# Moving low halves of probabilities to GpSimd, and LayerNorm's centring and the scaling of cumulated sums to ScalarE

## The chip, the cores and the metric

The kernel runs on one core of a Trainium2 chip. A core has five engines that work at the same time, each through its own queue of instructions in the order of the program: TensorE (matmuls, PE in the profile, and PEld for the loading of its weights), VectorE (DVE), ScalarE (ACT), GpSimd (POOL) and SyncE (SP, which here issues nearly all DMAs). An instruction that has to wait for another engine holds up everything behind it on its own engine. The metric is the time of one execution on the device in microseconds (us).

## The reference

Three blocks follow each other. The shapes are 4 batches, 8 heads, 576 positions, 64 numbers per head, so a model width of 512; the hidden width of both MLPs is 2048.

```python
# attention, with a bias from cumulated sums
cum = cumsum(maximum(s, 0))
scores = q @ k.T / 8 + minimum(-(cum[i] - cum[j]), 0), causal
x = softmax(scores) @ v                                  # [4, 576, 512]
# first MLP, after a two-dimensional Fourier transform
u = x + real(fft(fft(x, axis=1), axis=2))
x = u + relu(layernorm(u) @ w_ch1) @ w_ch2
# second MLP
x = x + relu((layernorm(x) * g_ln) @ w_ch1') @ w_ch2'
```

Where the kernel needs more accuracy than fp16 has, it splits an fp32 value into two fp16 numbers: a high half (the value rounded) and a low half (what is left). A product of two such values is then three fp16 matmuls.

## The kernel before, in words

**Stages.** Attention of batch 0 runs first, beside the loading of the first MLP's weights. Then the first MLP works through the batches while the attention and the Fourier transform of the next batch are mixed into it: `Side` hands out pieces of the next batch's work after each step of the MLP. In the profile, MLP of batch 0 runs from about 169 to 308 us beside attention of batch 1, MLP of batch 1 from 310 to 450 beside attention of batch 2, MLP of batch 2 from 460 to 604 beside attention of batch 3, and MLP of batch 3 until about 727 beside the loading, converting and splitting of the second MLP's weights. From there on the second MLP runs alone; it uses a scheme with seven products in place of eight, for which GpSimd makes sums of activations (L461 to L464).

**Attention.** A batch has four pairs of heads; a pair has five tiles of query rows (`A0`, `A1`, `M`, `B1`, `B0`, numbers 0, 1, 2, 3, 4) for each of two heads, 40 units a batch. A tile reaches back over 129, 257, 320, 448 or 576 columns. A unit goes through the engines like this (batches 2 and 3):

- GpSimd writes the masked bias into the unit's fp32 tile (`emit_bias`, L739), three units ahead. It reads the pair's cumulated sums, spread over all rows and multiplied by the pair's scale (`scale_cum`, L655).
- TensorE makes the scores in PSUM (L756, L757; the PSUM pool has three slots), and VectorE adds them to the bias and finds the minimum of a row (L758), which frees the slot.
- ScalarE takes the exponential twice: as fp16, the high half (L781), and as fp32 in place with the sum of a row (L782).
- VectorE or GpSimd subtracts one from the other, which is the low half (`emit_lo`, L794). `KN["LO_POOL"]` lists for each batch the tiles that GpSimd takes; VectorE takes the others. The fp32 tile is free after that, for the bias of a later unit.
- SyncE issues a DMA that transposes both halves (L798, L806), and TensorE multiplies them with v (`emit_pv`, L826), five to seven units after the scores.

**LayerNorm.** `emit_ln` prepares a chunk of one or two tiles of 128 rows for an MLP: mean and variance (L338, L339), a rough reciprocal root `p` (L343), then for each tile the normalized row `un` in fp32, its high half, its low half, and a transposing DMA (L359). A finer factor for the root is applied to the MLP's output. `un` lies in buffers shared with attention; from the second MLP's weights on it has one buffer of its own. The next chunk's LayerNorm is mixed into the steps of the current chunk.

**Order.** A planner orders the instructions of each engine by a simulated time that it works out from costs of its own, by the order of the program and by priorities (`urgent`). All waits between engines follow from the data.

Of the kernel before, what the change touches and what calls it, by code (L numbers as in the profile page):

```python
# [26 lines left out]
EXT = [129, 257, 320, 448, 576]  # L27
NKB = [2, 3, 3, 4, 5]
MASKED = -(2.0 ** 120)
KN = {'PVS': (0, 3, 0, 0), 'ORD': ((0, 0, 0), (0, 0, 0), (1, 0, 0), (1, 0, 0)), 'WR4': (1.2, 1.2, 1.2, 1.2), 'W0': 4, 'WRATE': 1.0, 'W2PRE': 18, 'NCONST': 40, 'HOLDN': 1, 'S1': 4, 'S2': 1, 'S1B': 0, 'COST': (1.0, 1.0, 1.0, 1.0, 1.0), 'POOL1': (), 'POOLB': (0, 1, 2, 3, 4, 5, 6, 7), 'QF': (3, 3, 3, 3, 3, 3, 3, 3, 3, 3, 3), 'QL': (1, 1, 1, 1), 'WCALLS': 2, 'WN': 65, 'SPGATE': 0, 'LATE4': 1, 'MARK': 30, 'CJ': (2, 6), 'PVLAG': 7, 'LOLAG': 1, 'PVLAG32': 5, 'PJ32': 4, 'A0OFF': 0, 'A1OFF': 0, 'F0OFF': 300, 'AOFF': (200, 0, 300, 300), 'FOFF': (300, 600, 300, 150), 'LNOFF': (300, 600, 150, 600), 'LOFF': 300, 'PJ': 1, 'PN': 1, 'PL': 6, 'KPREP': 0, 'KPRE': (6, 0, 0), 'KSTEP': ((0, 0, 1), (0, 1), (1,)), 'RATES': (1.9, 1.4, 2.1, 1.2), 'POOLX': (0, 1, 1, 1), 'LO_POOL': ((0, 4, 1, 3, 2), (0, 1, 2, 3), (4,), (0, 1, 2)), 'TAILW': 2, 'LNM': 0, 'LAZY': 8, 'CALLS3': 65, 'N32': 2}  # L30


@with_exitstack
def fused_kernel(ctx: ExitStack, tc, q, k, v, s, wa1, wa2, g_ln, wb1, wb2, tok_c, feat_c, ident_c, rev_c, bias_c, out):
    nc = tc.nc
# [4 lines left out]
    mpool = ctx.enter_context(tc.tile_pool(name="mpool", bufs=2))  # L40
# [70 lines left out]
    class Weights:  # L111
# [42 lines left out]
        def convert(self, i):  # L154
# [172 lines left out]
    def emit_ln(ch):  # L327

        n = ch.n
        xs = [ch.get(j) for j in range(n)]
        ch.x = xs
        mv = small.tile([128, 2, 2], F32, tag="mv", name="mv")[:, 0:n, :]
        for j in range(n):
            st = small.tile([128, 6], F32, tag="st", name="st")
            nc.vector.bn_stats(out=st, in_=xs[j])  # L338
            nc.vector.bn_aggr(out=mv[:, j, :], in_=st)  # L339
        va4 = small.tile([128, 8], F32, tag="va", name="va")  # L340
        va, p, d, mp = (va4[:, 2 * i:2 * i + n] for i in range(4))
        nc.vector.tensor_scalar(out=va, in0=mv[:, :, 1], scalar1=1e-6, scalar2=None, op0=ALU.add)
        nc.vector.tensor_scalar(  # L343
            out=p.bitcast(I32), in0=va.bitcast(I32), scalar1=-0.5, scalar2=float(0x5F3759DF), op0=ALU.mult, op1=ALU.add
        )
        ch.last = nc.vector.scalar_tensor_tensor(out=mp, in0=mv[:, :, 0], scalar=-1.0, in1=p, op0=ALU.mult, op1=ALU.mult)
        yield
        ch.unT = mpool.tile([128, 8, 256], F16, tag="unT", name="unT")
        for j in range(n):
            un = un_tile[0]()[:, 0:512]  # L350
# [161 lines left out]
    class MlpStream:  # L512
# [5 lines left out]
        def run(self, chunks, side, first_ln=True, last=None):  # L518

            if first_ln:  # L520
                for _ in emit_ln(chunks[0]):
                    pass
            for c, ch in enumerate(chunks):
                nxt = urgent(emit_ln(chunks[c + 1]), KN["LOFF"]) if c + 1 < len(chunks) else None
                seven = isinstance(ch.w, Weights7)
                for m in range(MB // 2) if seven else range(0, MB, 2):
                    if not seven:
                        ch.w.lazy(m)
                    self.pend.append((ch, m, (emit_g1x if seven else emit_g1)(ch, m)))
# [773 lines left out]
    if True:  # L1303
# [59 lines left out]
        for n, _ in enumerate(urgent(emit_ln(first[0]), KN["LNOFF"][0])):  # L1363
            weights_after((list(KN["QL"]) + [0] * 9)[n], first[0].last)
# [110 lines left out]
```

## Time and profile before

| | |
|---|---|
| time, median of three runs | 1094.59 us (1094.49 to 1094.82) |
| the profiled execution's own time | 1095.33 us |
| its span, first to last instruction | 1093.6 us |
| mean granted TensorE clock | 0.95 of full speed |
| TensorE busy | 967.2 us, 8644 matmuls |
| VectorE busy | 720.1 us, 1848 instructions |
| ScalarE busy | 580.1 us, 1350 instructions |
| GpSimd busy | 415.3 us, 717 instructions |

The profile shows one execution. Busy time is time in which an engine worked on an instruction; issuing DMAs and waiting do not count. Matmuls overlap in a pipeline and their ends are modelled, so TensorE can be shown busy while it is not at its peak. The time that an engine sat idle before an instruction is put down to the instruction or DMA that came last among those it waited for. Times in a timeline are counted from the start of the span.

### The profile page before, as it was taken

The page shows a single profiled execution, that of the slowest core. Times are in us where ns is not written, and L with a number is a line of the kernel's source. Part 1 is how long each engine was busy: PE and PEld are TensorE (multiplying, and loading weights), DVE is VectorE, ACT ScalarE, POOL GpSimd, SP SyncE. Part 2 cuts the span into 40 slices and gives each one's busy share as a digit, 9 for nine tenths or more (in the row PEclk, how much of TensorE's full clock was granted, in tenths as well). Part 3 has the DMA queues.
Part 4 walks back from the last instruction along what each step waited for, and adds up shares of the span by engine and source line. Part 5 has one row for each costly group of instructions (what it writes and reads, how often), then busy time and mean ns, then how long its engine had stood idle before and what let it go on. Part 6 is the DMA issues. An engine that isn't in the chain of part 4 may idle for free.

```text
span 1093.6 us, 23078 instructions
## 1 busy us (share of the span) xinstructions
PE 967.2 (88%) x8644; PEld 740.8 (68%) x8644; DVE 720.1 (66%) x1848; ACT 580.1 (53%) x1350; POOL 415.3 (38%) x717
## 2 busy tenths in 40 slices
PE   4676379999888899688999998898999999999998
PEld 3454246776665666455766665576888888888887
DVE  5978998656896664965757599867644644552342
ACT  5778559774776653576622255744333334333341
POOL 3425444544242231323311000467545443543452
PEclk9768578999999999898999999999999999999999
DMA  6999956986579980598904297020211111110000
GB/s 177 277 199 264 241 132 136 177 147 132 112 139 204 167 157 1 122 196 138 190 20 151 68 291 252 21 58 1 59 20 47 52 27 53 40 40 20 20 21 21
DMA packets 291369, 125.48 MB, mean 115 GB/s; under 512 B 272952, under 2 KB 273208, under 8 KB 291256
## 3 DMA queue, kind: packets, MB, share of 16 engines
q1 hardware_dynamic: 290616, 121.90, 49.9%
q0 software_dynamic: 640, 2.10, 0.6%
q8 instruction: 68, 1.11, 0.4%
q14 instruction: 45, 0.37, 0.1%
HBM read 61.50 MB, written 9.51 MB: 65 GB/s over the span
## 4 chain that ended last, share of the span: by engine, by line
PE 38%; DVE 10%; POOL 3%; DMA 2%; ACT 1%; issue 1%; SPq 1%; ACTq 0%
PE acc L481 13%; PE g1x L453 7%; PE g L453 7%; PE g L387 4%; PE g L411 4%; POOL wbsums L304 2%; DVE wbbig L313 1%; DVE wbbig L165 1%; DMA wbbig<-in_moe_w_ch_dram 1%; DVE wbbig L162 1%; PE pv L826 1%; DVE h L394 1%; DVE wb L162 1%; DVE wb L165 1%; SPq L798 1%
## 5 line engine op out<-in xcount | busy, mean ns | idle before, releaser
L387 PE MATMUL g<-unT,wa 128*128 128x256 f16 (+1 forms) x1920 | 219.4, 265 | 1.4 <-DVE h L394 0.8
L411 PE MATMUL g<-wa,h 128*128 128x512 f16 x864 | 207.4, 382 | 9.2 <-DVE h L394 5.1
L387 PEld LDWEIGHTS <-wa 128*128 128x128 f16 x1920 | 173.9, 99 | 39.7 <-issue 3.0
L481 PE MATMUL acc<-wbbig,wa 128*128 128x256 f16 x1512 | 178.5, 273 | 6.6 <-DVE wa L467 5.3
L453 PEld LDWEIGHTS <-wb 128*128 128x128 f16 x1728 | 169.1, 98 | 20.2
L467 DVE TENSOR_TENSOR wa<-wa,wa 128x896 f16<-128x896 f32 x72 | 79.2, 1100 | 149.2 <-ACT wa L466 149.2
L481 PEld LDWEIGHTS <-wa 128*128 128x128 f16 x1512 | 147.3, 98 | 25.7 <-DVE wa L467 6.7
L411 PEld LDWEIGHTS <-h 128*128 128x128 f16 x864 | 82.9, 99 | 92.5 <-DVE h L394 8.6
L466 ACT CAST wa<-wa 128x896 f16<-128x896 f32 x72 | 67.4, 938 | 117.3 <-POOL wa L464 117.3
L794 POOL TENSOR_TENSOR p<-sc,p 128x129 f16<-128x129 f32 (+4 forms) x104 | 94.7, 917 | 82.6 <-ACT sc L782 74.8
L781 ACT ACTIVATE p<-sc,mn 128x576 f16<-128x576 f32 (+4 forms) x160 | 90.2, 576 | 58.6 <-DVE mn L1023 16.4
L826 PE MATMUL pv<-v,pT 128*128 128x64 f16 x1632 | 72.8, 202 | 43.4 <-DMA pT<-p 24.0
L826 PEld LDWEIGHTS <-pT 128*128 128x128 f16 x1632 | 66.9, 104 | 62.3 <-DMA pT<-p 31.5
L739 POOL TENSOR_SCALAR_AFFINE_SELECT sc<-cumb 128x129 f32<-128x129 f32 (+4 forms) x120 | 67.4, 573 | 109.7 <-DVE p L794 40.6
L453 PE MATMUL g1x<-unT,wb 128*128 128x256 f16 x864 | 101.5, 273 | 0.0
L453 PE MATMUL g<-unT,wb 128*128 128x256 f16 x864 | 100.9, 273 | 0.0
L463 POOL TENSOR_TENSOR wa<-wa 128x128 f32<-128x128 f32 x72 | 46.2, 642 | 121.2 <-ACT wa L460 121.2
L782 ACT ACTIVATE sc<-sc,mn 128x576 f32<-128x576 f32 (+4 forms) x160 | 91.6, 573 | 1.1
L1018 PE MATMUL s<-qkT 128*128 128x288 f32 (+4 forms) x192 | 74.1, 487 | 3.1 <-DVE wasc L106 1.4
L394 DVE SCALAR_TENSOR_TENSOR h<-g,h 128x512 f16<-128x512 f32 (+1 forms) x80 | 50.6, 633 | 38.0 <-ACT h L393 37.6
L393 ACT ACTIVATE h<-g 128x512 f16<-128x512 f32 (+1 forms) x80 | 43.5, 544 | 59.8 <-PE g L387 59.3
L775 POOL MEMSET p<- 128x128 f16 x64 | 13.0, 204 | 112.5 <-DMA pT<-p 80.3
(224 smaller groups left out, 1536.6 us busy)
## 6 DMA issues: line engine op xcount, KB each, us to landing
wbbig<-in_moe_w_ch_dram SPq DMA_DIRECT2D x32, 512.0 KB
wa<-in_moe_w_ch_dram SPq DMA_DIRECT2D x21, 512.0 KB
cumb<-cumd SPq DMA_DIRECT2D x24, 288.0 KB
xset<-in_moe_w_ch_dram SPq DMA_DIRECT2D x11, 512.0 KB
x2d<-o SPq DMA_DIRECT2D x18, 256.0 KB
raw<-in_v_dram SPq DMA_DIRECT2D x32, 128.0 KB
out_dram<-wa SPq DMA_DIRECT2D x16, 256.0 KB
raw<-in_q_dram SPq DMA_DIRECT2D x48, 64.0 KB
```

What stands on the lines that cost most here:

```text
L387: nc.tensor.matmul(out=ps[:, c * i:c * i + c], lhsT=ch.w.w1(lw, kk, m + i), rhs=ch.unT[:, 4 * lx + kk, 0:c], start=(n == 0), stop=(n == 23),)
L411: nc.tensor.matmul(out=ch.ps[j], lhsT=h[:, lh, c:c + 128], rhs=ch.w.w2(lw, m + i), start=(m + i + n == 0), stop=(m + i == MB - 1 and n == 2),)
L453: nc.tensor.matmul(out=ps, lhsT=ch.w.w1(lw, kk, m + 8 * half), rhs=ch.unT[:, 4 * lx + kk, :], start=(n == 0), stop=(n == 11),)
L466: nc.scalar.copy(out=h[:, 0], in_=r[:, 0:7])
L467: nc.vector.tensor_tensor(out=h[:, 1], in0=r[:, 0:7], in1=h[:, 0], op=ALU.subtract)
L481: nc.tensor.matmul(out=acc[key], lhsT=h[:, lh, ia], rhs=b[:, ib, lw], start=(m == 0 and i == 0 and not second), stop=(m == 7 and i == 2 an ...
L739: nc.gpsimd.affine_select(out=u.f[:, 0:n], in_=P.cumb[u.h][:, 0:n], pattern=[[-1, n]], compare_op=ALU.is_ge, fill=MASKED, base=base, chann ...
L781: nc.scalar.activation(out=u.w[:, 0:n], in_=u.f[:, 0:n], func=AF.Exp, bias=mn, scale=-1.0)
L782: nc.scalar.activation(out=u.f[:, 0:n], in_=u.f[:, 0:n], func=AF.Exp, bias=mn, scale=-1.0, accum_out=u.rs[:, h:h + 1])
L794: eng.tensor_tensor(out=u.w[:, w:w + n], in0=u.f[:, 0:n], in1=u.w[:, 0:n], op=ALU.subtract)
L826: nc.tensor.matmul(out=ps[:, c], lhsT=pT[:, lp * nb + kb, :], rhs=P.v[:, kb, lv, c], start=(n == 0), stop=(n == 3 * nb - 1),)
L1018: nc.tensor.matmul(out=ps, lhsT=P.qT[:, QCOLS[t]], rhs=P.kT[h][:, a:z], start=not pe, stop=not masked,)
```

## The change

Three edits. `LO_POOL` now lists all five tiles for batches 2 and 3, where it listed only number 4 for batch 2 and 0, 1, 2 for batch 3; for batch 0 it lists the same five in another order. In `emit_ln`, ScalarE subtracts the mean into `un`, ScalarE multiplies it by `p` into the high half, and VectorE multiplies and subtracts for the low half; VectorE made a normalized `un` before. `mp` is now the negative mean alone. In `scale_cum`, ScalarE scales the cumulated sums in place of VectorE.

```diff
-'LO_POOL': ((0, 4, 1, 3, 2), (0, 1, 2, 3), (4,), (0, 1, 2))
+'LO_POOL': ((0, 1, 2, 3, 4), (0, 1, 2, 3), (0, 1, 2, 3, 4), (0, 1, 2, 3, 4))
...
-        ch.last = nc.vector.scalar_tensor_tensor(out=mp, in0=mv[:, :, 0], scalar=-1.0, in1=p, op0=ALU.mult, op1=ALU.mult)
+        ch.last = nc.vector.tensor_scalar(out=mp, in0=mv[:, :, 0], scalar1=-1.0, scalar2=None, op0=ALU.mult)
...
             un = un_tile[0]()[:, 0:512]
-            nc.vector.tensor_scalar(
-                out=un, in0=xs[j], scalar1=mv[:, j, 0:1], scalar2=p[:, j:j + 1], op0=ALU.subtract, op1=ALU.mult
-            )
+            nc.scalar.activation(out=un, in_=xs[j], func=AF.Identity, scale=1.0, bias=mp[:, j:j + 1])
             u16 = mpool.tile([128, 1024], F16, tag="u16", name="u16")
-            nc.scalar.activation(
-                out=u16[:, 0:512], in_=xs[j], func=AF.Identity, scale=p[:, j:j + 1], bias=mp[:, j:j + 1]
-            )
-            ch.last = nc.vector.tensor_tensor(out=u16[:, 512:1024], in0=un, in1=u16[:, 0:512], op=ALU.subtract)
+            nc.scalar.activation(out=u16[:, 0:512], in_=un, func=AF.Copy, scale=p[:, j:j + 1])
+            ch.last = nc.vector.scalar_tensor_tensor(
+                out=u16[:, 512:1024], in0=un, scalar=p[:, j:j + 1], in1=u16[:, 0:512], op0=ALU.mult, op1=ALU.subtract
+            )
...
     def scale_cum(p, h):
         P = pairs[p]
-        nc.vector.tensor_scalar(out=P.cumb[h], in0=P.cumb[h], scalar1=P.sc[:, 6:7], scalar2=None, op0=ALU.mult)
+        nc.scalar.activation(out=P.cumb[h], in_=P.cumb[h], func=AF.Copy, scale=P.sc[:, 6:7])
```

## Rows read from the trace of the kernel before

**Rows 1.** The page, busy time, share of the span and instructions of each engine.

```profile
PE 967.2 (88%) x8644; PEld 740.8 (68%) x8644; DVE 720.1 (66%) x1848; ACT 580.1 (53%) x1350; POOL 415.3 (38%) x717
```

**Rows 2.** Busy time by stage: start:end, length, busy us (instructions), clock, DMA.

```profile
175.00:250.00 75.00, 74.56 (x714) 52.91 (x712) 51.63 (x167) 63.59 (x167) 39.82 (x74) 1.00 0.82 152
250.00:425.00 175.00, 155.24 (x1486) 109.63 (x1483) 123.21 (x367) 101.10 (x250) 55.20 (x101) 0.99 0.74 138
425.00:475.00 50.00, 38.04 (x274) 24.00 (x273) 36.65 (x137) 27.91 (x72) 18.38 (x35) 0.90 0.54 103
475.00:575.00 100.00, 92.29 (x1043) 66.68 (x1040) 62.81 (x184) 55.51 (x146) 30.09 (x58) 0.97 0.71 130
...
650.00:700.00 50.00, 41.42 (x353) 27.41 (x351) 45.76 (x108) 29.93 (x70) 10.88 (x8) 0.97 0.58 179
...
790.00:1094.00 304.00, 297.51 (x2724) 266.18 (x2722) 132.94 (x241) 110.47 (x199) 131.71 (x247) 1.00 0.12 32
```

**Rows 3.** TensorE's waits, 250-575: line, releaser, us in total, times, longest.

```profile
PE s L756 <- DVE mn L758: 16.8, 11, 8.8
PE pv L826 <- DMA pT<-p: 9.7, 7, 3.4
```

**Rows 4.** Timelines of GpSimd and TensorE, 449-458: start, us, instruction [idle before, releaser].

```profile
449.58 0.47 POOL L739 TENSOR_SCALAR_AFFINE_SELECT sc<-cumb 128x129 f32<-128x129 f32 x1 [5.40 <-DVE cumb L655]
450.02 1.82 POOL L794 TENSOR_TENSOR p<-sc,p 128x257 f16<-128x257 f32 x1
...
452.42 1.94 POOL L794 TENSOR_TENSOR p<-sc,p 128x320 f16<-128x320 f32 x1
...
454.69 0.79 POOL L794 TENSOR_TENSOR p<-sc,p 128x320 f16<-128x320 f32 x1
455.44 1.48 POOL L739 TENSOR_SCALAR_AFFINE_SELECT sc<-cumb 128x320 f32<-128x320 f32 x3
...
457.53 0.40 PE L756 MATMUL s<-qkT,qx 128*128 128x288 f16 x1 [8.77 <-DVE mn L758]
```

**Rows 5.** Low halves, groups by line: count | busy, mean ns | idle before.

```profile
L794 DVE TENSOR_TENSOR p<-sc,p 128x576 f16<-128x576 f32 (+4 forms) x56 | 34.3, 620 | 6.6 <-ACT sc L782 6.4
...
L794 POOL TENSOR_TENSOR p<-sc,p 128x129 f16<-128x129 f32 x8 | 4.0, 500 | 9.0 <-ACT sc L782 8.9
L794 POOL TENSOR_TENSOR p<-sc,p 128x257 f16<-128x257 f32 x8 | 6.9, 870 | 1.0 <-ACT sc L782 0.8
L794 POOL TENSOR_TENSOR p<-sc,p 128x320 f16<-128x320 f32 x8 | 7.4, 936 | 5.9 <-ACT sc L782 5.9
L794 POOL TENSOR_TENSOR p<-sc,p 128x448 f16<-128x448 f32 x16 | 19.1, 1191 | 14.7 <-ACT sc L782 14.5
L794 POOL TENSOR_TENSOR p<-sc,p 128x576 f16<-128x576 f32 x8 | 10.6, 1324 | 8.1 <-ACT sc L782 8.1
```

**Rows 6.** Passes of LayerNorm, of weights' splitting and the sums' scaling, by line.

```profile
L355 ACT ACTIVATE u<-xset,va 128x512 f16<-128x512 f32 x34 | 26.7, 806 | 23.1 <-DMA unT<-u 16.0 <-DVE va L346 6.5 <-DVE va L362 0.4
L358 DVE TENSOR_TENSOR u<-un,u 128x512 f16<-128x512 f32 x36 | 25.5, 709 | 8.2 <-ACT u L355 7.7
L204 DVE SCALAR_TENSOR_TENSOR wa<-wa,wasc,wa 128x512 f16<-128x512 f32 x30 | 24.6, 823 | 1.8 <-ACT wa L203 1.7
L203 ACT ACTIVATE wa<-wa,wasc 128x512 f16<-128x512 f32 x30 | 21.0, 710 | 3.9 <-DVE wa L204 2.1 <-DVE wasc L106 1.6
L351 DVE TENSOR_SCALAR un<-xset,mv,va 128x512 f32<-128x512 f32 x34 | 21.0, 624 | 0.3
L655 DVE TENSOR_SCALAR cumb<-cumb,scs 128x576 f32<-128x576 f32 x16 | 8.1, 515 | 11.1 <-DMA cumb<-cumd 11.1
```

**Rows 7.** Timeline of TensorE, the first matmuls of batch 1's MLP.

```profile
309.95 1.81 PE L387 MATMUL g<-unT,wa 128*128 128x256 f16 x15 [0.69 <-DMA unT<-u]
```

**Rows 8.** GpSimd's waits, 250-575.

```profile
POOL sc L739 <- DVE p L794: 40.6, 19, 5.7
POOL sc L739 <- DVE cumb L655: 30.7, 8, 7.3
```

More of the change, by code (lines that the diff above doesn't have):

```diff
@@ L29 @@
 MASKED = -(2.0 ** 120)
-KN = {'PVS': (0, 3, 0, 0), 'ORD': ((0, 0, 0), (0, 0, 0), (1, 0, 0), (1, 0, 0)), 'WR4': (1.2, 1.2, 1.2, 1.2), 'W0': 4, 'WRATE': 1.0, 'W2PRE': 18, 'NCONST': 40, 'HOLDN': 1, 'S1': 4, 'S2': 1, 'S1B': 0, 'COST': (1.0, 1.0, 1.0, 1.0, 1.0), 'POOL1': (), 'POOLB': (0, 1, 2, 3, 4, 5, 6, 7), 'QF': (3, 3, 3, 3, 3, 3, 3, 3, 3, 3, 3), 'QL': (1, 1, 1, 1), 'WCALLS': 2, 'WN': 65, 'SPGATE': 0, 'LATE4': 1, 'MARK': 30, 'CJ': (2, 6), 'PVLAG': 7, 'LOLAG': 1, 'PVLAG32': 5, 'PJ32': 4, 'A0OFF': 0, 'A1OFF': 0, 'F0OFF': 300, 'AOFF': (200, 0, 300, 300), 'FOFF': (300, 600, 300, 150), 'LNOFF': (300, 600, 150, 600), 'LOFF': 300, 'PJ': 1, 'PN': 1, 'PL': 6, 'KPREP': 0, 'KPRE': (6, 0, 0), 'KSTEP': ((0, 0, 1), (0, 1), (1,)), 'RATES': (1.9, 1.4, 2.1, 1.2), 'POOLX': (0, 1, 1, 1), 'LO_POOL': ((0, 4, 1, 3, 2), (0, 1, 2, 3), (4,), (0, 1, 2)), 'TAILW': 2, 'LNM': 0, 'LAZY': 8, 'CALLS3': 65, 'N32': 2}
+KN = {'PVS': (0, 3, 0, 0), 'ORD': ((0, 0, 0), (0, 0, 0), (1, 0, 0), (1, 0, 0)), 'WR4': (1.2, 1.2, 1.2, 1.2), 'W0': 4, 'WRATE': 1.0, 'W2PRE': 18, 'NCONST': 40, 'HOLDN': 1, 'S1': 4, 'S2': 1, 'S1B': 0, 'COST': (1.0, 1.0, 1.0, 1.0, 1.0), 'POOL1': (), 'POOLB': (0, 1, 2, 3, 4, 5, 6, 7), 'QF': (3, 3, 3, 3, 3, 3, 3, 3, 3, 3, 3), 'QL': (1, 1, 1, 1), 'WCALLS': 2, 'WN': 65, 'SPGATE': 0, 'LATE4': 1, 'MARK': 30, 'CJ': (2, 6), 'PVLAG': 7, 'LOLAG': 1, 'PVLAG32': 5, 'PJ32': 4, 'A0OFF': 0, 'A1OFF': 0, 'F0OFF': 300, 'AOFF': (200, 0, 300, 300), 'FOFF': (300, 600, 300, 150), 'LNOFF': (300, 600, 150, 600), 'LOFF': 300, 'PJ': 1, 'PN': 1, 'PL': 6, 'KPREP': 0, 'KPRE': (6, 0, 0), 'KSTEP': ((0, 0, 1), (0, 1), (1,)), 'RATES': (1.9, 1.4, 2.1, 1.2), 'POOLX': (0, 1, 1, 1), 'LO_POOL': ((0, 1, 2, 3, 4), (0, 1, 2, 3), (0, 1, 2, 3, 4), (0, 1, 2, 3, 4)), 'TAILW': 2, 'LNM': 0, 'LAZY': 8, 'CALLS3': 65, 'N32': 2}
 @with_exitstack
@@ L350, in emit_ln @@
             un = un_tile[0]()[:, 0:512]
-            nc.vector.tensor_scalar(
-                out=un, in0=xs[j], scalar1=mv[:, j, 0:1], scalar2=p[:, j:j + 1], op0=ALU.subtract, op1=ALU.mult
-            )
-            u16 = mpool.tile([128, 1024], F16, tag="u16", name="u16")
-            nc.scalar.activation(
-                out=u16[:, 0:512], in_=xs[j], func=AF.Identity, scale=p[:, j:j + 1], bias=mp[:, j:j + 1]
-            )
-            ch.last = nc.vector.tensor_tensor(out=u16[:, 512:1024], in0=un, in1=u16[:, 0:512], op=ALU.subtract)
+            nc.scalar.activation(out=un, in_=xs[j], func=AF.Identity, scale=1.0, bias=mp[:, j:j + 1])
+            u16 = mpool.tile([128, 1024], F16, tag="u16", name="u16")
+            nc.scalar.activation(out=u16[:, 0:512], in_=un, func=AF.Copy, scale=p[:, j:j + 1])
+            ch.last = nc.vector.scalar_tensor_tensor(
+                out=u16[:, 512:1024], in0=un, scalar=p[:, j:j + 1], in1=u16[:, 0:512], op0=ALU.mult, op1=ALU.subtract
+            )
             ch.tr = nc.sync.dma_start_transpose(out=ch.unT[:, :, j * 128:(j + 1) * 128], in_=u16)
```

## The prediction

> **What bounds the kernel now.** I read the page first, then busy time by stage, then TensorE's waits, then the queue of the engine that is to get more work. The page [rows 1] gives TensorE 88% busy, VectorE 66%, ScalarE 53%, GpSimd 38%. No share of a whole span says what a change in one stage is worth, so the stages come next [rows 2]: in 175-250 TensorE is busy 74.56 of 75 us and from 790 on 297.51 of the 303.6 that are left. Nothing done to another engine shortens those; it can only spoil them. Between 250 and 575, where attention of batches 2 and 3 runs beside the first MLP's matmuls, TensorE is not busy for 175 - 155.24, 50 - 38.04 and 100 - 92.29 us, 39.4 together, and in 650-700 for 8.6. That is all the room there is to win, and the place where it can grow. In 250-575 no other engine is full: VectorE 222.7, ScalarE 184.5, GpSimd 103.7 of 325 us. The lost time is therefore latency and order in queues, not throughput. TensorE's waits there [rows 3] are led by the score PSUM slots that VectorE's add-and-minimum (L758) must empty, 16.8 us in 11 waits, one of them 8.8, and by transposed probabilities that have not landed, 9.7 us in 7.
>
> The one wait of 8.77 us looks like VectorE's, but its queue shows otherwise [rows 4]: GpSimd waits 5.40 us for a scaled cumulated sum, then runs in its own order a bias (0.47), a low half of 1.82, biases, a low half of 1.94, another of 0.79, and only then, at 455.44 and after, the biases one of which is the wide one that L758 needs. TensorE goes on at 457.53. Low halves are 4.55 us of that hole. GpSimd is far from full, and still its order sets the end of the largest hole of this stage.
>
> **The change part by part.** *Low halves (L794).* 48 instructions leave VectorE: of batch 2 the four narrower tiles (129, 257, 320 and 448 columns), of batch 3 those of 448 and 576, eight each. Batch 0's entry lists the same five tiles in another order and changes nothing. On VectorE they cost 48 x 0.620 = 29.8 us; on GpSimd, by the means of the same widths [rows 5], 8 x (0.500 + 0.870 + 0.936 + 1.191) = 28.0 for batch 2 and 8 x (1.191 + 1.324) = 20.1 for batch 3, 48.1 us together. GpSimd then has 151.8 of 325 us (47%), VectorE falls by 29.8. What this does to the end has three terms.
>
> First, relief. L758 queues behind VectorE's other work; without the 8.77 that is GpSimd's, its ten other waits are 8.0 us. They vanish at best, and stay if it is the scores or ScalarE that are late. VectorE loses nearly a fifth of its work here (42 of 222.7 with the edits below), and a queue's waits shrink by more than its load: I take -3 between -8.0 and 0.
>
> Second, GpSimd's order. Each low half now stands between biases, and waits in that queue for ScalarE's second exponential while the next units' biases stand behind it; VectorE's scores wait for those. Batch 2 has had only its 576-wide low halves there. It now gets what made the hole of batch 3, and batch 3 gets its two widest added (2 x (1.191 + 1.324) = 5.0 us a head pair). Price: the 4.55 us of low halves in a hole of the measured kind, once more at batch 2, and little at batch 3, since the planner may put the wide ones where the queue has slack. Bounds 0 and +17.5 (a hole of 8.77 in either batch); I take +5, nearest to the 4.55.
>
> Third, a low half is later by 48.1 / 48 - 0.62 = 0.4 us on average, and its transposing DMA with it. Seven waits for such DMAs would grow by 0 to 0.5 each: 0 to +3.5, of which I take +1.5, as matrix products are issued five to seven units later and most have slack.
>
> A rule speaks to the price on GpSimd. The rows show two low halves of 320 columns, one of 1.94 us and one of 0.79, in one queue three microseconds apart [rows 4]. The Trainium skill (GPSIMD Engine Reference, Key points) says that GpSimd shares its SBUF interfaces with VectorE and contends with VectorE's instructions that use two ports or have two SBUF inputs. The two rows fit that and do not prove it, as what VectorE ran beside them is not among the rows. By that rule taking 48 two-input passes off VectorE speeds up those that are left on GpSimd, to 0.79 of a mean of 0.936, a sixth, some 7 of the 48.1 us (an estimate), and the sum below would be 0.7 us lower.
>
> *LayerNorm's centring.* Before, VectorE made the normalized row (L351, 0.624) while ScalarE made its fp16 half from the input (L355, 0.806), and VectorE subtracted (L358, 0.709). After, ScalarE centres, then scales, each with one per-row operand, as L203 at 0.710 [rows 6], and VectorE multiplies and subtracts in one pass, as L204 at 0.823. A tile costs ScalarE 2 x 0.710 - 0.806 = +0.61 and VectorE 0.823 - 0.709 - 0.624 = -0.51; over 36 tiles +22 and -18 us. The small negation of the mean costs the same as the product it replaces. What counts is the chain of the two-tile chunk that opens a batch's MLP: from 2 x 0.806 + 0.709 = 2.32 us to 4 x 0.710 + 0.823 = 3.66, +1.34. Batch 1 has nothing in front of it: its first matmul waited for this chunk's transposing DMA [rows 7], so +1.34. Batch 0's chunk also feeds the first matmuls of its MLP, with some attention to fill in: +1.0. Batch 2's lies beside the 8.77 hole and ends with it: +0.7 of 1.34. Batch 3's is ready over ten microseconds ahead: 0. In 650-700 VectorE is busy 45.76 of 50 with converting weights, which I take for the cause of TensorE's 8.6: four tiles at -0.51 give back 2.0 at most, I take -1.5. From 790 on the normalization is a chunk ahead of TensorE, which covers it; yet there the centred row has one buffer, so ScalarE's second centring newly waits for VectorE's subtraction of the first tile, with the activations' relu and cast behind it on ScalarE and TensorE behind those. A chunk goes to 2 x (0.710 + 0.710 + 0.823) = 4.49 us, +2.2; a step's 45 matmuls take 45 x 297.51 / 2724 = 4.9 us there [rows 2] and two steps stand between, so 0. Without that cover it would be up to 2.2 for each of some eight chunks. Sum of the edit: +1.5, between -1 and +5.
>
> *Cumulated sums.* Sixteen passes of 0.515 on VectorE become passes of 576 columns on ScalarE, estimated from 0.710 for 512 as 0.71 to 0.80: +12 us on ScalarE, -8.2 on VectorE. GpSimd's first bias of a pair waits for it (30.7 us in all [rows 8]); behind exponentials on ScalarE it can come later than behind VectorE's work, or sooner. It is 0.25 us longer; two a batch stand before a hole. I take 0, between -2 and +4.
>
> The sum: -3 + 5 + 1.5 + 1.5 + 0 = +5. The profiled execution took 1095.33 (span 1093.6 and 1.7 around it), 0.74 above the median of the runs, 1094.59; so 1100.3 by the profile and **1099.6** by the median.
>
> **Rivals.** *GpSimd freed.* Of GpSimd's waits in 250-575, 40.6 us are for low halves on VectorE, whose buffer the next bias overwrites, and 30.7 for VectorE's scaling [rows 8]. With the low half on the same queue the first kind is gone, biases come sooner, and holes like that at 457 shrink. For it: GpSimd is idle two thirds of the stage, and in 175-250, with four of five low halves there, TensorE is full. Against it: that stage has heavier fp32 score matmuls to cover, and the buffer's wait becomes one for ScalarE. All of the 8.0 and half the hole, 4.4, with the normalization's +1.5: -11, 1084 to 1091.
>
> *Off the path.* Matrix products lag scores by five to seven units, and each term above is under a quarter of the lag; then the normalization and the relief cancel and the time is 1092.4 to 1096.8. What I call the same is within 0.2%, 2.2 us, about what a measurement of this kernel can tell. Against it: the rows show that the slots wait now.
>
> *Pile-up.* GpSimd's queue falls behind in both batches, or ScalarE, blocked by its new wait, gives relus late. The point from which it decides is a bias later than the three score slots allow, which the hole shows to be near: +17.5, 1108 to 1115.
>
> One uncertainty has no row: the planner orders each engine by its own costs, and with other costs the mix of MLP and attention on TensorE can differ from 160 us on, either way by a few microseconds. It widens every case.
>
> **Chances.** Forecast (slower by 2.2 to 13 us) 0.50, freed 0.22, off the path 0.17, pile-up 0.11. So faster 0.22, same 0.17, slower 0.61. The range leaves out most of the freed case and the upper part of the pile-up: 1089 to 1112.
>
> **What would show it.** Right: in 250-575 VectorE near 180 busy us and GpSimd near 150; TensorE's unused time there above 39.4, with long waits at L756 whose releaser, followed through L758, is a bias behind low halves; a gap of some 2 us before the first matmul of batch 1's MLP. Wrong: TensorE's unused time falls, GpSimd's waits for low halves are not replaced by waits for ScalarE, or the time moves after 790, where I put nothing.

## The result, and the profile after

The changed kernel takes 1083.67 us (median of 6 runs, 1082.76 to 1088.68) against 1094.54 us for the kernel before (6 runs, same chip): a ratio of 0.990, 95% interval 0.9885 to 0.9915, 10.9 us less. The forecast was 5 us more. The profiled execution took 1084.09, with a span of 1082.3. From L359 on, lines stand two lower than before: L792 is the low half, L653 the scaling of the sums, L756 the add-and-minimum.

The page of the changed kernel, the row that answers to [rows 1]:

```profile
PE 962.1 (89%) x8644; PEld 737.9 (68%) x8644; DVE 674.9 (62%) x1748; ACT 610.8 (56%) x1402; POOL 454.9 (42%) x765
```

Its busy time by stage, as [rows 2]:

```profile
250.00:425.00 175.00, 161.67 (x1565) 113.92 (x1562) 109.12 (x325) 111.44 (x271) 76.82 (x136) 1.00 0.73 139
425.00:475.00 50.00, 37.68 (x264) 23.73 (x264) 36.95 (x132) 31.43 (x77) 21.84 (x39) 0.83 0.61 126
475.00:575.00 100.00, 94.58 (x1064) 69.65 (x1062) 58.75 (x182) 59.87 (x154) 44.12 (x73) 0.98 0.66 119
650.00:700.00 50.00, 43.66 (x343) 28.70 (x342) 45.16 (x105) 34.61 (x75) 10.68 (x8) 0.97 0.42 136
```

TensorE's unused time in 250-575 falls from 39.4 to 13.33 + 12.32 + 5.42 = 31.1 us. Work has moved as the edits say: VectorE 222.7 to 204.8 us there, GpSimd 103.7 to 142.8, ScalarE 184.5 to 202.7. A fixed window holds different work in two kernels that run at different speeds, so where the gain arises is read from the times at which the same matmuls run. The first matmuls of the MLPs of batches 2 and 3, then of the second MLP, in the kernel before:

```profile
459.88 1.01 PE L387 MATMUL g<-unT,wa 128*128 128x256 f16 x4
...
606.96 0.49 PE L387 MATMUL g<-unT,wa 128*128 128x256 f16 x3
...
723.71 0.38 PE L453 MATMUL g<-unT,wb 128*128 128x256 f16 x2
```

and, in the changed kernel, the same with the first of batch 1 ahead of them:

```profile
310.24 0.94 PE L385 MATMUL g<-unT,wa 128*128 128x256 f16 x7 [0.74 <-DMA unT<-u]
...
454.70 0.82 PE L385 MATMUL g<-unT,wa 128*128 128x256 f16 x3 [1.23 <-DMA unT<-u]
...
599.54 0.49 PE L385 MATMUL g<-unT,wa 128*128 128x256 f16 x3
...
715.09 0.38 PE L451 MATMUL g<-unT,wb 128*128 128x256 f16 x2
```

At 310 nothing is gained (before, the first one there began at 309.95 [rows 7]); 5.2 us are at batch 2's MLP, 7.4 at batch 3's, 8.6 at the second MLP, and the spans differ by 11.3. Two thirds arise in 310-600, where two batches' attention runs beside the MLP. The second MLP itself, from its first matmul to the end, takes 367.2 us in place of 369.8.

TensorE's waits in 250-575, as [rows 3], and GpSimd's, as [rows 8]:

```profile
PE s L754 <- DVE mn L756: 11.2, 5, 7.1
PE pv L824 <- DMA pT<-p: 7.5, 8, 2.6
...
POOL p L792 <- ACT sc L780: 51.5, 23, 6.4
POOL sc L737 <- ACT cumb L653: 30.8, 12, 10.5
```

The 40.6 us for which biases waited for VectorE's low halves are gone. Low halves' waits for ScalarE's exponentials, before,

```profile
POOL p L794 <- ACT sc L782: 23.7, 10, 6.3
```

grew to 51.5, as the forecast wrote, and TensorE does not wait longer: its waits for L756 are 5.6 us shorter. The large hole is still there. GpSimd, VectorE and TensorE around it, as [rows 4]:

```profile
445.40 1.95 POOL L737 TENSOR_SCALAR_AFFINE_SELECT sc<-cumb 128x129 f32<-128x129 f32 x3 [4.52 <-ACT cumb L653]
448.21 0.67 POOL L737 TENSOR_SCALAR_AFFINE_SELECT sc<-cumb 128x576 f32<-128x576 f32 x1 [0.86 <-DVE f L366]
448.85 1.43 POOL L792 TENSOR_TENSOR p<-sc,p 128x257 f16<-128x257 f32 x2
...
450.56 0.51 DVE L756 CUSTOM_DVE_ANT_0 sc<-s,sc,scs 128x288 f32<-128x288 f32 x1
450.60 0.79 POOL L792 TENSOR_TENSOR p<-sc,p 128x320 f16<-128x320 f32 x1
...
451.13 0.40 PE L754 MATMUL s<-qkT,qx 128*128 128x288 f16 x1 [7.07 <-DVE mn L756]
```

It went from 8.77 to 7.07 us, and GpSimd's low halves no longer set its end: the wide bias (448.21) now runs ahead of all three of them and is written by 448.88. VectorE takes the add-and-minimum 1.7 us later, at 450.56, without having stood idle. Low halves on GpSimd in 250-575, as [rows 5],

```profile
L792 POOL TENSOR_TENSOR p<-sc,p 128x576 f16<-128x576 f32 x16 | 21.2, 1336 | 8.8 <-ACT sc L780 6.8 <-issue 1.9
L792 POOL TENSOR_TENSOR p<-sc,p 128x448 f16<-128x448 f32 x16 | 16.7, 1048 | 11.9 <-ACT sc L780 11.9
L792 POOL TENSOR_TENSOR p<-sc,p 128x320 f16<-128x320 f32 x18 | 14.4, 804 | 2.6 <-ACT sc L780 2.6
L792 POOL TENSOR_TENSOR p<-sc,p 128x257 f16<-128x257 f32 x16 | 10.7, 681 | 6.8 <-ACT sc L780 6.7
L792 POOL TENSOR_TENSOR p<-sc,p 128x129 f16<-128x129 f32 x16 | 7.4, 464 | 23.5 <-ACT sc L780 23.5
```

(The 448-column row of [rows 5] is from batches 0 and 1, before 272 us; in 250-575 VectorE made those low halves.) LayerNorm's passes and the scaling, as [rows 6], cost about what was worked out:

```profile
L354 DVE SCALAR_TENSOR_TENSOR u<-un,va,u 128x512 f16<-128x512 f32 x36 | 30.6, 851 | 20.6 <-ACT u L353 20.6
L353 ACT ACTIVATE u<-un,va 128x512 f16<-128x512 f32 x36 | 25.4, 713 | 8.8 <-DMA unT<-u 8.7
L351 ACT ACTIVATE un<-xset,va 128x512 f32<-128x512 f32 x34 | 24.0, 717 | 26.7 <-DVE va L346 13.0 <-DVE u L354 6.6 <-POOL p L792 3.0
L653 ACT ACTIVATE cumb<-cumb,scs 128x576 f32<-128x576 f32 x16 | 11.9, 765 | 4.9 <-DMA cumb<-cumd 4.9
```

So the costs of these passes were forecast well and the time was not. The last row leads on: the scaling waits for the DMA that loads the sums, now on ScalarE, 4.9 us. Before, VectorE stood still for 11.1 us at that point; the figure is in [rows 6], and the forecast did not use it.

### The profile page after: what moved, and what is told of

Read it like the earlier page. It is cut to its first block, busy times and chain, and to the rows that moved or that the text cites. A ratio compares the mean times of both kernels' runs of the same rounds, so it can differ in the third digit from the quotient of the medians.

```text
span 1082.3 us, 23115 instructions
## 1 busy us (share of the span) xinstructions
PE 962.1 (89%) x8644; PEld 737.9 (68%) x8644; DVE 674.9 (62%) x1748; ACT 610.8 (56%) x1402; POOL 454.9 (42%) x765
## 4 chain that ended last, share of the span: by engine, by line
PE 36%; DVE 8%; POOL 3%; DMA 1%; issue 1%; ACT 1%; DVEq 0%; ACTq 0%; POOLq 0%
PE acc L479 13%; PE g1x L451 7%; PE g L451 7%; PE g L385 4%; PE g L409 4%; POOL wbsums L304 1%; DMA wbbig<-in_moe_w_ch_dram 1%; DVE wbbig L165 1%; DVE wbbig L162 1%; DVE st L338 1%; DVE h L392 1%; DVE wb L165 1%; DVE wb L162 1%; DVE wbbig L159 0%; PE y L1124 0%
## 5 line engine op out<-in xcount | busy, mean ns | idle before, releaser
L792 POOL TENSOR_TENSOR p<-sc,p 128x448 f16<-128x448 f32 (+4 forms) x152 | 135.7, 904 | 119.6 <-ACT sc L780 109.2
L465 DVE TENSOR_TENSOR wa<-wa,wa 128x896 f16<-128x896 f32 x72 | 80.3, 1115 | 145.6 <-ACT wa L464 145.6
L409 PEld LDWEIGHTS <-h 128*128 128x128 f16 x864 | 82.4, 98 | 91.3 <-DVE h L392 10.8
L779 ACT ACTIVATE p<-sc,mn 128x129 f16<-128x129 f32 (+4 forms) x160 | 89.8, 575 | 35.7 <-DVE mn L1021 17.6
L461 POOL TENSOR_TENSOR wa<-wa 128x128 f32<-128x128 f32 x72 | 49.9, 693 | 116.1 <-ACT wa L458 116.1
L780 ACT ACTIVATE sc<-sc,mn 128x129 f32<-128x129 f32 (+4 forms) x160 | 91.5, 573 | 0.9
L737 POOL TENSOR_SCALAR_AFFINE_SELECT sc<-cumb 128x129 f32<-128x129 f32 (+4 forms) x120 | 64.4, 551 | 50.6 <-ACT cumb L653 30.8
L201 POOL TENSOR_TENSOR wb<-wb,wb 128x512 f16<-128x512 f32 x8 | 10.7, 1355 | 111.3 <-DVE wbbig L165 106.0
```

The costliest lines, as they stand in the source:

```text
L409: nc.tensor.matmul(out=ch.ps[j], lhsT=h[:, lh, c:c + 128], rhs=ch.w.w2(lw, m + i), start=(m + i + n == 0), stop=(m + i == MB - 1 and n == 2),)
L465: nc.vector.tensor_tensor(out=h[:, 1], in0=r[:, 0:7], in1=h[:, 0], op=ALU.subtract)
L737: nc.gpsimd.affine_select(out=u.f[:, 0:n], in_=P.cumb[u.h][:, 0:n], pattern=[[-1, n]], compare_op=ALU.is_ge, fill=MASKED, base=base, chann ...
L779: nc.scalar.activation(out=u.w[:, 0:n], in_=u.f[:, 0:n], func=AF.Exp, bias=mn, scale=-1.0)
L780: nc.scalar.activation(out=u.f[:, 0:n], in_=u.f[:, 0:n], func=AF.Exp, bias=mn, scale=-1.0, accum_out=u.rs[:, h:h + 1])
L792: eng.tensor_tensor(out=u.w[:, w:w + n], in0=u.f[:, 0:n], in1=u.w[:, 0:n], op=ALU.subtract)
```

## Experiments

The theories. A: freed queues, so the low halves carry the gain. B: no edit owns it; each edit makes the planner find another order, and the time moves with the order. C: VectorE's load counts. D, formed after the first four runs: VectorE waits for the sums' DMA with the scaling at the head of its queue, and the add-and-minimum passes behind it, on which TensorE depends, wait too; on ScalarE the wait harms little.

Each kernel was timed beside the kernel before on its own chip (medians of before 1093.38 to 1094.56); the ratios are against that, the differences in the text against 1094.54.

| kernel | median us | ratio to before, 95% interval | VectorE's wait for the sums' DMA, 250-575 |
|---|---|---|---|
| before | 1094.54 | | 11.1 |
| e1_low, low halves alone | 1091.10 | 0.9956 to 0.9979 | 9.5 |
| e2_ln, LayerNorm alone | 1088.48 | 0.9928 to 0.9959 | 11.7 |
| e3_cum, scaling alone | 1085.13 | 0.9904 to 0.9931 | none |
| e4_low2, low halves of batch 2 alone | 1094.01 | 0.9981 to 1.0013 | 11.9 |
| e8_cumln, scaling and LayerNorm | 1087.88 | 0.9924 to 0.9962 | none |
| e9_cumlow, scaling and low halves | 1085.30 | 0.9895 to 0.9942 | none |
| e14_lowln, low halves and LayerNorm | 1088.75 | 0.9945 to 0.9973 | 8.3 |
| changed, all three | 1083.67 | 0.9885 to 0.9915 | none |
| e10_head, scaling moved, wait put back | 1098.57 | 1.003 to 1.0064 | 14.7 |
| e11_load, scaling moved, passes early | 1100.27 | 1.004 to 1.0088 | none |
| e12_load2, scaling moved, load put back | 1087.12 | 0.992 to 0.996 | none |
| e7_pool, scaling on GpSimd | 1087.71 | 0.993 to 0.9966 | none |
| e13_null, before and idle copy | 1090.38 | 0.9959 to 0.9988 | 5.4 |
| e15_null_b2, before and idle copy | 1092.38 | 0.9972 to 0.9996 | 6.2 |
| e16_null_b3, before and idle copy | 1083.72 | 0.9898 to 0.9936 | 6.1 |
| e19_null_b4, before and idle copy | 1084.74 | 0.989 to 0.9933 | 6.0 |
| e17_null_cum, scaling moved and idle copy | 1088.77 | 0.9933 to 0.9966 | none |
| e18_null_all, changed and idle copy | 1086.47 | 0.9917 to 0.9956 | none |
| e20_null_all2, changed and idle copy | 1082.57 | 0.987 to 0.9917 | none |

### One part alone

The diffs are those of the change, one edit each. For e1_low and e4_low2:

```diff
-'LO_POOL': ((0, 4, 1, 3, 2), (0, 1, 2, 3), (4,), (0, 1, 2))
+'LO_POOL': ((0, 1, 2, 3, 4), (0, 1, 2, 3), (0, 1, 2, 3, 4), (0, 1, 2, 3, 4))   # e1_low
+'LO_POOL': ((0, 4, 1, 3, 2), (0, 1, 2, 3), (0, 1, 2, 3, 4), (0, 1, 2))         # e4_low2
```

> Only the low halves move (batches 2 and 3). Theory A, freed queues: nearly all of the 10.9 us came from here, because GpSimd no longer waits for VectorE's low half and VectorE has 28 us less to do: -8 to -11 us. Theory B, the planner's order: the gain belongs to no edit, and this one alone gives anything between -5 and +5. Theory C, lighter VectorE at LayerNorm and the sums: this one gives -2 to 0. My forecast's price for GpSimd's order (+5) would show here as 0 to +5.

-3.4 us. A falls: the low halves don't carry the gain.

> Only the low halves of batch 2 move; batch 3 stays as before. Theory A: the time falls where batch 2's attention runs, -5 to -8 us, since the changed kernel's MLP of batch 1 ended 7.7 us earlier. Theory B: -5 to +5 and not at the same place. Forecast: 0 to +5.

No difference. This tests the largest term of the forecast, GpSimd's order at batch 2: the same 32 low halves are put into the queue. TensorE's stages in e4_low2, and its waits for VectorE's add-and-minimum in 250-575:

```profile
250.00:425.00 175.00, 155.35 (x1469) 109.97 (x1470) 113.97 (x333) 100.64 (x249) 78.89 (x133) 0.98 0.72 137
425.00:475.00 50.00, 44.13 (x322) 27.61 (x321) 38.41 (x135) 30.43 (x76) 17.45 (x35) 0.97 0.55 113
475.00:575.00 100.00, 88.43 (x991) 63.68 (x990) 63.26 (x183) 54.48 (x144) 31.50 (x59) 0.95 0.68 126
...
PE s L756 <- DVE mn L758: 9.8, 8, 3.0
```

In 250-425, batch 2's stretch, GpSimd has 23.7 us more work than before [rows 2] and TensorE is as busy as before (155.35 against 155.24). No second hole came, and the first one is gone: the longest of these waits is 3.0 us. Batch 2's MLP begins 3.1 us earlier than before (456.77 against 459.88), and this is lost again by batch 3's (607.95 against 606.96), whose low halves are as before.

e2_ln has LayerNorm's edit alone:

> Only LayerNorm's centring moves to ScalarE. Forecast: +1.5 (from -1 to +5), from +1.34 us of chain at the first chunk of a batch's MLP. Theory A: +1 to +3. Theory B: -5 to +5. Theory C: -3 to -8, as VectorE has 18 us less to do, 1.5 to 2 of it in 650-700.

-6.1 us, where the forecast had +1.5 in a range of -1 to +5. e3_cum has the scaling alone:

> Only the scaling of the cumulated sums moves to ScalarE. Forecast 0 (from -2 to +4). Theory A: -1 to +1. Theory B: -5 to +5. Theory C: -2 to -5.

-9.4 us, more than any theory gave. The three parts sum to 18.9 us, the whole gave 10.9: they are not additive. This is VectorE in the kernel before at such a place (start, us, instruction, idle before):

```profile
350.35 0.52 DVE L655 TENSOR_SCALAR cumb<-cumb,scs 128x576 f32<-128x576 f32 x1 [3.09 <-DMA cumb<-cumd]
350.82 0.58 DVE L758 CUSTOM_DVE_ANT_0 sc<-s,sc,mn 128x288 f32<-128x288 f32 x1
```

The scaling stands at the head for 3.09 us, with an add-and-minimum right behind it. There are six such waits, 11.1 us. In e3_cum VectorE has none and ScalarE waits for that DMA for 2.2 us. That is where D comes from. How much of it reaches TensorE can be read from the same trace. Behind three of the six, at 350.35, 379.68 and 480.36, TensorE then waits for the add-and-minimum:

```profile
351.45 0.27 PE L756 MATMUL s<-qkT 128*128 128x257 f16 x1 [0.78 <-DVE mn L758]
...
381.21 0.27 PE L756 MATMUL s<-qkT 128*128 128x257 f16 x1 [1.26 <-DVE mn L758]
...
481.37 0.27 PE L756 MATMUL s<-qkT 128*128 128x257 f16 x1 [1.04 <-DVE mn L758]
```

These are 3.1 us together. So the chain of D stands in the trace, but directly it covers a third of the 9.4.

### The wait, or the load

e10_head leaves the scaling on ScalarE and lets VectorE read one column of the sums first; the copy is used by nothing.

```diff
+nc.vector.tensor_copy(out=small.tile([128, 1], F32, tag="hw", name="hw"), in_=P.cumb[h][:, 0:1])
 nc.scalar.activation(out=P.cumb[h], in_=P.cumb[h], func=AF.Copy, scale=P.sc[:, 6:7])
```

> The scaling of cumulated sums on ScalarE, alone, took 1085.13 (0.9918 of before). Here it stays on ScalarE, and VectorE gets back, at the same place of the program, one copy of a single column of the sums as they land: 16 instructions of about 0.08 us in place of 16 of 0.515, so VectorE has the wait for the sums' DMA at the head of its queue again, without the load of the passes. Theory D (head of the queue: while VectorE waits for that DMA, 11.1 us before, the add-and-minimum passes behind it wait too): VectorE's waits for the sums come back, 7 to 13 us, and most of the gain goes, 1091 to 1096. Theory C (VectorE's load: it is the 8.2 us of passes that count): the gain stays, 1084 to 1087. Theory B (only the order that the planner finds): anything within 5 of 1090, with no link to the waits.

The copies cost little and wait long (groups by line: busy, mean ns, idle before):

```profile
L655 DVE COPY hw<-cumb 128x1 f32<-128x1 f32 x16 | 2.4, 152 | 25.8 <-DMA cumb<-cumd 25.6
```

1098.57: all of the scaling's gain goes, and 4 us more than that. C, with the load gone, expected 1084 to 1087; D expected the loss, but only to 1091 to 1096, with waits of 7 to 13 us. The run does not put the old waits back. Of the 25.6 us, 14.7 lie in 250-575, and 10.8 lie before 250, where the kernel before has none:

```profile
DVE hw L655 <- DMA cumb<-cumd: 10.8, 3, 5.3
```

And in 250-575, where D would look for the loss, TensorE's waits for L758 are short:

```profile
PE s L756 <- DVE mn L758: 3.6, 4, 1.4
```

So the run agrees with D in direction and does not show its chain.

e11_load has a reduction over constants in place of the copy:

```diff
+nc.vector.tensor_reduce(out=small.tile([128, 1], F32, tag="hw", name="hw"), in_=ones.to_broadcast([128, 576]), op=ALU.max, axis=AX)
```

> The scaling on ScalarE, and on VectorE at the same place a reduction over 576 repeated constants, which waits for nothing: some 0.5 to 0.7 us each, 16 times, so VectorE has the load of the passes again without the wait. Its result is unused. Theory D: VectorE has no wait for the sums' DMA and the gain stays but for a trifle, 1084 to 1088. Theory C: the gain goes with the load, 1091 to 1095. Theory B: anything within 5 of 1090.

This one failed as an experiment: having nothing to wait for, the 16 reductions were ordered into the first 18 us, where they delay batch 0 (its MLP begins at 177.3 us, before at 169.4):

```profile
2.29 2.00 DVE L655 TENSOR_REDUCE hw<-ones 128x1 f32<-128x576 f32 x3
```

e12_load2 ties them to the pair's scale:

```diff
+nc.vector.tensor_reduce(out=small.tile([128, 1], F32, tag="hw", name="hw"), in_=P.sc[:, 6:7].to_broadcast([128, 400]), op=ALU.max, axis=AX)
```

> e11_load's question again: there the planner moved the 16 reductions to the first 17 us of the kernel, as they waited for nothing at all. Here they read the pair's scale, which VectorE itself makes shortly before the passes of the kernel before stood, so they fall in 250-575. By e11's duration (0.736 for 576) some 0.51 each for 400, like a pass. The scaling is on ScalarE. Theory D (the wait at the head of VectorE's queue cost the time): 1084 to 1088. Theory C (VectorE's load): 1091 to 1095. Theory B (the planner's order): anything within 5 of 1090.

```profile
L655 DVE TENSOR_REDUCE hw<-scs 128x1 f32<-128x400 f32 x16 | 8.4, 559 | 0.0
```

VectorE has 8.4 us of passes again, as before (8.1), without the wait, and 7 of the 9.4 us of gain stay. C expected 1091 to 1095 and missed. e7_pool scales on GpSimd:

```diff
-nc.vector.tensor_scalar(out=P.cumb[h], in0=P.cumb[h], scalar1=P.sc[:, 6:7], scalar2=None, op0=ALU.mult)
+nc.gpsimd.tensor_scalar(out=P.cumb[h], in0=P.cumb[h], scalar1=P.sc[:, 6:7], scalar2=None, op0=ALU.mult)
```

> The kernel before with the scaling on GpSimd, whose biases are the only readers of the scaled sums. The wait for the DMA then blocks GpSimd alone, which would wait for the sums anyway; a pass costs GpSimd an estimated 0.7 to 1.3 us (its passes over 576 columns: bias 0.67 in the trace, low half 1.32), 11 to 21 us in all. Theory D: VectorE is relieved of the wait as on ScalarE; GpSimd's low halves behind the waiting pass come later, which costs a part: 1085 to 1090. Theory C: as far as VectorE's load goes the same, -2 to -5, and GpSimd's extra load costs some of it: 1090 to 1094. Theory B: within 5 of 1094.5.

```profile
L655 POOL TENSOR_SCALAR cumb<-cumb,scs 128x576 f32<-128x576 f32 x16 | 30.9, 1935 | 25.4 <-DVE scs L670 16.1 <-DVE va L362 3.0 <-DVE rs L904 2.2
```

GpSimd pays 30.9 us for it, and the kernel is still 6.8 us quicker than before, within what D gave. Two results inside D's ranges and one in its direction; yet each also has another order, so the pairs and the controls had to follow.

### Two parts

> The scaling on ScalarE and LayerNorm's edit together, the low halves as before. Alone they took 9.3 and 5.9 us off (1085.13, 1088.48); with the low halves' 3.5 the three sum to 18.7, and the whole change gave 10.9. If the two act in different stretches (sums in 250-575; LayerNorm's at the first matmul of a batch's MLP and in 650-790) they add up: 1079 to 1082. If they remove the same waits, 1083 to 1086, like the whole change. If it is the low halves that cost the rest once the other two are in, this kernel beats the changed one by 3 or more.

> Low halves and scaling without LayerNorm's edit (alone -3.5 and -9.3). Additive: 1081 to 1083, which would beat the changed kernel. If both work on the same waits in 250-575: 1084 to 1087. With cumulated sums and LayerNorm together at 1087.88, above the sums alone, a result of 1081 to 1083 would say that LayerNorm's edit costs where the queues are already free.

> The whole change without the scaling: that pass stays on VectorE. Theory D: the wait for the sums' DMA is back at the head of VectorE's queue, some 10 us of it, and most of the gain goes: 1089 to 1093. Theory C: the low halves' and LayerNorm's relief of VectorE (30 and 18 us against 8) carries nearly all of it: 1084 to 1087. Additive of the parts alone: 1085.

1087.88 (above all of its cases), 1085.30 (that of the same waits) and 1088.75 (just under D's 1089, above C's 1087). With the scaling in, neither of the other parts by itself adds anything; without it, the two together give no more than LayerNorm alone. The scaling is worth 9.4 us alone, 5.8 on top of the low halves, 5.1 on top of the other two and 0.6 on top of LayerNorm. A part with one mechanism and one price would not behave like that.

### Edits that do nothing

A copy of the pair's scale, one column, unused, is added at the scaling. It was put ahead of it on VectorE (e13_null, e17_null_cum, e18_null_all), behind it on VectorE (e15_null_b2), ahead of it on ScalarE (e16_null_b3, e20_null_all2) and behind it on ScalarE (e19_null_b4).

```diff
+nc.vector.tensor_copy(out=small.tile([128, 1], F32, tag="hw", name="hw"), in_=P.sc[:, 6:7])   # e13, e15, e17, e18
+nc.scalar.copy(out=small.tile([128, 1], F32, tag="hw", name="hw"), in_=P.sc[:, 6:7])          # e16, e19, e20
```

> The kernel before, with a copy of the pair's scale (one column, result unused) on VectorE ahead of each of the 16 scaling passes: nothing that costs more than 0.15 us each, 2.4 us of VectorE's time in all, and no new wait. It shows how far the planner's order alone moves the time. Theories C and D: within 2 of before. Theory B: it can move by 3 to 10 either way.

> The kernel before with a copy of the pair's scale (one column, unused) on VectorE behind each of the 16 scaling passes, not ahead of them as in e13_null. Theory D (the wait for the sums' DMA in VectorE's queue decides): VectorE's wait for it stays between 5 and 12 us, and the time between 1090 and 1097, going with the wait. Theory B (the planner's order decides): the time has no link to that wait and can come out at 1084 to 1088, like the kernels with the scaling moved.

> The kernel before with the same unused copy on ScalarE, ahead of each scaling pass, which stays on VectorE. Theories as for e15_null_b2: D 1090 to 1097 with a wait of 5 to 12 us, B anything from 1084 to 1100.

> The scaling on ScalarE (1085.13 alone), with the unused copy on VectorE ahead of it; it reads the pair's scale, not the sums, and so has no wait for the DMA. It differs from e10_head, at 1098.57, in what the copy reads. Theory D: no wait for the sums in VectorE's queue, 1083 to 1088. Theory B: it can be anywhere up to 1098.

> The whole change (1083.67) with the same unused copy on VectorE. Theory D: 1081 to 1087. Theory B: within 6 of 1086 either way.

> The kernel before with the unused copy on ScalarE behind each scaling pass, not ahead of it as in e16_null_b3 (1083.72). So far the kernels with the wait in VectorE's queue lie at 1083.7 to 1098.6 (mean 1091), those without at 1083.7 to 1088.8 (mean 1086.5). Theory B alone: anywhere from 1084 to 1099. Theory D as a part of some 5 us on top of the order: above 1088 in three cases of four.

> The whole change with the unused copy on ScalarE ahead of each scaling pass. Theory D as a part on top of the order: 1082 to 1089, as the others without the wait in VectorE's queue. Theory B alone: it can come out above 1090.

e16_null_b3 is the run that decides. Sixteen copies on ScalarE, none of them used, take as much off the kernel before as the whole change. The copies, by line:

```profile
L655 ACT COPY hw<-scs 128x1 f32<-128x1 f32 x16 | 2.2, 181 | 0.0
```

Its wait for the sums in 250-575, and the hole in its timeline:

```profile
DVE cumb L655 <- DMA cumb<-cumd: 6.1, 4, 1.9
```

```profile
451.76 0.40 PE L756 MATMUL s<-qkT,qx 128*128 128x288 f16 x1 [9.50 <-DVE mn L758]
```

The copies take 2.2 us in all, VectorE still waits 6.1 us for the sums (of 11.1), and the hole is longer than before, 9.50. None of this explains the gain: e13_null and e15_null_b2 have waits of 5.4 and 6.2 and take 1090.38 and 1092.38, and e10_head and e4_low2, without the hole, take 1098.57 and 1094.01. What differs is the order. TensorE around 264 us in the kernel before, and the same place in e16_null_b3:

```profile
263.73 1.24 PE L411 MATMUL g<-wa,h 128*128 128x512 f16 x5
264.81 0.98 PE L1126 MATMUL y<-tok,eo 128*128 128x320 f16 x6
265.62 1.24 PE L411 MATMUL g<-wa,h 128*128 128x512 f16 x5
```

```profile
262.74 1.46 PE L411 MATMUL g<-wa,h 128*128 128x512 f16 x6
264.04 0.98 PE L1126 MATMUL y<-tok,eo 128*128 128x320 f16 x6
264.85 1.03 PE L411 MATMUL g<-wa,h 128*128 128x512 f16 x4
```

Up to here both have the same matmuls in the same order; from here on one matmul of the MLP stands ahead of six of the Fourier transform, and everything behind follows its own course. The traces hold a sharper test. In e16_null_b3 and e19_null_b4 all four engines run the same instructions in the same order, but for the idle copies, ahead of the scaling in one and behind it in the other: they take 1083.72 and 1084.74. e13_null and e15_null_b2 differ from each other in 16 of 12559 places, and take 1090.38 and 1092.38. With the order kept, the time moves by 1 to 2 us; between the two orders, by 6 to 9.

B is right that the order alone moves this kernel by the size of the result. D's expectations of no change within 2 us for e13 and of 1090 to 1097 for e16 fell, and so did its three in four for e19 (1084.74); e17 came out just above its range. What stays of D is the nearest pair: e10_head and e17_null_cum differ only in what the 16 copies read, the arriving sums or a number that is there, and take 1098.57 and 1088.77, though in two orders.

What is left for the edits? Kernels that differ by idle copies alone: before, 1094.54, 1090.38, 1092.38, 1083.72, 1084.74, mean 1089.2; changed, 1083.67, 1086.47, 1082.57, mean 1084.2. All kernels but e10 and e11 (left out with their results known; with them the difference is 1.3), with the scaling on VectorE (nine, mean 1089.8, standard deviation 3.8) and off it (nine, mean 1086.1, 2.1): 3.7 apart, with a standard error of sqrt(3.8²/9 + 2.1²/9) = 1.4. As e13 and e15 share an order, and e16 and e19, the kernel before has been seen in three orders and not five; with each pair counted once the 3.7 become 4.3, standard error 1.5, and the gap between the idle-copy means 5.8, standard error 3.3. So some 4 to 6 of the 10.9 us go with the edits and the rest with the kernel before standing at the slow end of its own orders. That split rests on few orders of each kernel and is an estimate. e20_null_all2, at 1082.57, is the quickest kernel here and can't be told from the changed one: the intervals overlap.

## Why the prediction was wrong

**The step that failed** is the second term of the low halves, GpSimd's order, +5, the largest of the sum: "the 4.55 us of low halves in a hole of the measured kind, once more at batch 2". No such hole came. e4_low2, which makes that edit for batch 2 alone, cost nothing and has no wait at L758 above 3.0 us, and the low halves alone gave -3.4 where the forecast's three terms sum to +3.5 (-3, +5, +1.5). Before, GpSimd's low halves did stand before the wide bias in the hole; in the changed kernel they stand behind it, and the 40.6 us for which biases had waited for VectorE's low halves [rows 8] went away. Nor was the hole a measure of the time: e16_null_b3 has the longest, 9.50, and is as quick as the changed kernel. The second failure is as large: the planner's order, left out of the sum, moves the kernel by as much as the whole result (below). The rival "GpSimd freed", at 1084 to 1091, by its sum of -11, came within 0.4 us of the time. That is in good part luck: the hole that it would have shortened by 4.4 lost 1.7, and the low halves alone gave a third.

**Cumulated sums**, 0 between -2 and +4: alone -9.4. The forecast looked at who waits for the scaled sums (GpSimd, 30.7 us [rows 8]) and not at what the scaling itself waits for and who stands behind it, though the 11.1 us stood in a row that it quoted [rows 6]. Part of the -9.4 is order: between the two groups above the scaling is worth 3.7 to 4.3, and TensorE's waits directly behind VectorE's are 3.1.

**LayerNorm**, +1.5 between -1 and +5: alone -6.1. The chain was worked out as instructions in a row, +1.34 at batch 1's first matmul. The gap there went from 0.69 to 0.74 us; presumably the longer chain is paid ahead of time. TensorE's busy time in 650-700 rose by 43.66 - 41.42 = 2.2 us (forecast 1.5), but not by this edit: e2_ln, with it alone, has 41.89, and e16_null_b3, without it, 44.61. What LayerNorm's edit does give comes later. From its first matmul to the end, the second MLP takes 367.1 to 367.6 us in the six kernels with the edit and 368.9 to 369.9 in the fourteen without it. These 2 us, nearly all won within its first 85, are the one part of the gain that comes with an edit in every order, and the forecast had nothing on that stretch. TensorE's waits for VectorE's L467 (L465 after), which prepares the second MLP's activations, in 575-790, before and after:

```profile
PE acc L481 <- DVE wa L467: 4.6, 3, 2.9
```

```profile
PE acc L479 <- DVE wa L465: 2.4, 4, 1.0
```

In 575-800 they are 2.0 to 2.4 in the six and 2.9 to 5.3 in the fourteen.

**Relief of VectorE**, -3 between -8.0 and 0: the waits at L756 fell by 5.6, inside the bounds, though e10_head, whose VectorE keeps its low halves, has only 3.6 us of them. **Later low halves**, +1.5: waits for transposed probabilities fell from 9.7 to 7.5. GpSimd's passes came out quicker than the old means, by 7 to 22% up to 448 columns (257 columns 0.870 to 0.681), not at 576; at their new means the 48 that moved cost 8 x (0.464 + 0.681 + 0.804 + 1.048) + 8 x (1.048 + 1.336) = 43.1 us against the 48.1 worked out. That can't be put down to passes that left VectorE. e13_null, whose VectorE keeps them all, has

```profile
L794 POOL TENSOR_TENSOR p<-sc,p 128x257 f16<-128x257 f32 x8 | 5.4, 686 | 6.3 <-ACT sc L782 5.0 <-issue 1.1
```

and the old mean of 0.870, over eight passes, holds the one of 1.82 [rows 4]. The rule of the Trainium skill (GPSIMD Engine Reference, Key points), that GpSimd contends with VectorE's two-input passes, is neither shown nor refuted here; that the 5.0 us are near the 7 of the estimate by it is no evidence.

**The uncertainty without a row.** The forecast said that the planner's order "widens every case" by "a few microseconds". That was the right place and the wrong size: seven idle copies moved their kernels by between -10.8 (e16) and +3.6 (e17) us. Terms of 1 to 5 us, added to a sign, could not be worth a chance of 0.61 for slower here.

**Of the signs named beforehand**: GpSimd near 150 (142.8) held; VectorE near 180 did not, it is at 204.8, 17.9 less than before of the 42 worked out (over the whole run it fell by 45.2), partly because the fixed window now reaches further into the run's work; TensorE's unused time above 39.4 and a gap near 2 us at batch 1's MLP were wrong. GpSimd's waits for low halves were replaced by waits for ScalarE as forecast, without TensorE waiting longer.

## What to carry to other kernels

Look in each engine's queue for an instruction that waits for a DMA at its head: its idle figure in the groups by line bounds what it can cost those behind it, whatever the instruction itself takes. What it does cost is read from the bottleneck's waits right behind it (here 3.1 of 11.1 us). The longest hole of a profile need not be what the time hangs on. Where a planner orders the queues, an edit of a few microseconds can't be judged from one order: add an instruction that does nothing, at several places, and see how far the time moves before giving the credit to the edit. Compare the orders too: controls that found the same order count as one. What holds across all orders, like the 2 us of the second MLP, can be credited. A sum of small terms then needs a chance near one half for either sign, however well each term is worked out.

## What was not expected of the hardware

A multiplication of 128x576 fp32 by a per-row number takes GpSimd 1.94 us, ScalarE 0.765 and VectorE 0.515, while GpSimd's bias over the same 576 columns takes 0.72 on average (16 in the kernel before). In the kernel before one low half of 257 columns took GpSimd 1.82 us and one of 320 took 1.94, another of 320 three microseconds later 0.79 [rows 4]. No run here shows why.
